# The first eight microseconds: two DMA queues, constant fillers, halved means and one tile turned by DMA instead of PE

## Chip, cores, metric

One core of a Trainium2 chip, one launch. The metric is the device time of a launch in microseconds; the median of several executions is quoted. The kernel takes about 1624 us, and the change touches only its opening, so everything below is about differences of 0.1 to 3 us.

## The reference

Four blocks in a row on x of 2048 x 1024 in bf16: linear attention, a gated bilinear block, and both again. Only the start matters here:

```python
x = A_x                                             # 2048 x 1024
x = x + _A_ref(_layernorm(x, axis=-1), A_wqkv, A_wo)
# _A_ref: qkv = x @ wqkv; phi(q), phi(k); ... ; o @ wo
```

The kernel cannot do its first useful product before a tile of 128 rows has been loaded, centred, and transposed, and the first slice of the k weights has landed.

## The kernel before

PE computes k = xn @ Wk for tiles of 128 rows; each tile needs 8 weight chunks of 128 rows (256 KB each) and 16 matmuls. Tiles 0 to 3 are the opening. Tile 0 gets its mean on VectorE, tile 1 on ScalarE. Tiles 0 to 2 are turned by PE transposes and copied from PSUM to `xT`; tile 3 is turned by a DMA. Until tile 0 is ready PE does "fillers": 9 matmuls on a zeroed tile, whose results nobody reads.

```python
for c in range(2):                                   # tile 0 in two halves of columns
    load(X[:, 0, c*NB:(c+1)*NB], x_view[:, 0, c*NB:(c+1)*NB])
load_x(1)
for k in range(2): load_k(k, k + 1)                  # k weights by chunks; load() is SyncE's queue
load_x(2)
...
nc.vector.memset(xT[3][:, 0, :], 0.0)
def idle(n):                                         # the fillers
    for _ in range(n):
        nc.tensor.matmul(out=zps[:, 0, :], lhsT=xT[3][:, 0, 0:P], rhs=xT[3][:, 0, :], ...)
... (cut)
idle(9)
ln_stats(0)                                          # 2 bn_stats + aggregate on VectorE
centre(0, stat[0][0][:, 0:1])
nc.scalar.activation(out=junk[:], in_=X[:, 1, :], func=ACT.Copy, scale=1.0/D, accum_out=mean1[:])
turn_pe(0, 2)
take(nc.vector.tensor_copy, 0, 0, 0, 2); take(nc.scalar.copy, 0, 1, 2, 8)
centre(1, mean1[:])
k_part(0, 0, 1)                                      # k_part(tile, first chunk, end chunk)
turn_pe(1, 4)
take(nc.vector.tensor_copy, 1, 0, 0, 4); take(nc.scalar.copy, 1, 1, 4, 8)
ln_stats(2); centre(2, ...)
k_part(1, 0, 1)
... (cut: chunks 1 and 2) ...
turn_pe(2, 8)
... (cut)
```

## Time and profile before

| what | value |
|---|---|
| median before the prediction, 3 executions | 1623.66 us (1623.5 to 1624.11) |
| all executions of this study but the profiled one, 50 of them | mean 1623.70 us (1623.1 to 1624.91) |
| the profiled execution | 1624.31 us, of which 1622.4 us is the span of its trace |

The first lines of the page of the kernel before. PE is the TensorE matmul row; a busy PE is not a PE at its peak (from 9 to 11 us, shown below, it reads 2.00 of 2.00 us busy with 17 instructions in one trace and with 7 in another).

```profile
span 1622.4 us, 18054 instructions
PE 1609.2 (99%) x7718; PEld 735.2 (45%) x7869; DVE 615.5 (38%) x941; ACT 283.8 (17%) x383; POOL 54.5 (3%) x135
```

So PE is the limit, and a change of the opening is worth what it moves PE's unbroken run forward. The chain of waits in the first 24 us says where that run begins. Columns: start us, us, what.

```profile
1.65 3.85 DMA X<-in_A_x_dram
...
5.51 1.16 ACT junk L422 x2
...
6.70 0.50 DVE R L398
...
7.24 0.41 PE pt L411 x4
...
7.68 0.44 DVE xT L414
...
8.16 2.33 PE ps L198 x10
10.49 0.45 PE pt L411 x8
```

Read it so: tile 1 of X (the DMA) landed at 5.49 us, ScalarE took its mean, VectorE centred it, PE turned it, VectorE copied it, and from 8.16 us PE does not wait again in this stretch. Tile 2's 8 transposes take 0.45 us of PE in the middle of that run.

PE's instructions in order of time in the same kernel (start us, us, line, operation, count, and in brackets the idle time before and what ended it):

```profile
1.17 4.02 PE L168 MATMUL ps<-xT 128*128 128x512 bf16 x9 [1.17 <-DVE xT L163]
5.17 0.68 PE L411 MATMUL pt<-ident,R 128*128 128x128 bf16 x8
6.23 0.59 PE L198 MATMUL ps<-W,xT 128*128 128x512 bf16 x2 [0.38 <-DMA W<-in_A_wqkv_dram]
7.24 0.62 PE L411 MATMUL pt<-ident,R 128*128 128x128 bf16 x8 [0.42 <-DVE R L398]
8.16 2.33 PE L198 MATMUL ps<-W,xT 128*128 128x512 bf16 x10 [0.30 <-DVE xT L414]
```

One thing is easily overlooked: the fillers start 0.427 us apart, the matmuls from 8.16 us on 0.216 us apart, with the same shape. PE's clock doubled in between; the trace's record of it is at 5.33 us, and there the distance of the transposes falls from 0.107 to 0.056 us.

### The profile page before, as it was taken

How to read it: one execution, taken by the hardware profiler on the slowest of the kernel's cores; microseconds unless marked ns; L12 is line 12 of the kernel's file. 1: busy time of each engine (PE TensorE's matmuls, PEld its weight loads, DVE VectorE, ACT ScalarE, POOL GpSimd, SP SyncE). 2: the span in 40 equal slices, each digit the busy share in tenths (PEclk: the TensorE clock that was granted, in tenths of full speed). 3: DMA queues.
4: the chain of work that ended last, by engine and by line, in shares of the span. 5: the costliest groups of instructions: out<-in, count | busy, mean ns of one | idle time of the engine just before them, and what ended most of it. 6: DMA issues, size and time to landing. Idle time of an engine off the chain costs nothing.

```text
span 1622.4 us, 18054 instructions
## 1 busy us (share of the span) xinstructions
PE 1609.2 (99%) x7718; PEld 735.2 (45%) x7869; DVE 615.5 (38%) x941; ACT 283.8 (17%) x383; POOL 54.5 (3%) x135
## 2 busy tenths in 40 slices
PE   9999999999999999999999999999999999999999
PEld 4444444444444444444444444444444444444444
DVE  6799853212311321243245798432123113211111
ACT  5523201101110110011045222011011101101110
POOL 2100000000000000010000000000000000000000
PEclk9999999999999999999999999999999999999999
DMA  7324856511650452142420349555235406511400
GB/s 233 59 72 98 241 162 175 162 53 55 167 168 0 141 160 89 52 155 63 90 56 1 78 98 252 156 163 163 71 101 172 130 20 175 162 65 65 156 0 26
DMA packets 235775, 182.84 MB, mean 113 GB/s; under 512 B 101296, under 2 KB 216496, under 8 KB 235696
## 3 DMA queue, kind: packets, MB, share of 16 engines
q1 hardware_dynamic: 235696, 181.69, 38.9%
q8 instruction: 61, 1.00, 0.3%
q14 instruction: 18, 0.15, 0.0%
HBM read 153.09 MB, written 4.19 MB: 97 GB/s over the span
## 4 chain that ended last, share of the span: by engine, by line
PE 99%; issue 1%; DMA 0%; DVE 0%; ACT 0%; SPq 0%
PE ps L198 50%; PE ps L529 47%; PE ps L556 1%; PE kv L312 0%; DMA X<-in_A_x_dram 0%; PE pm L337 0%; ACT junk L422 0%; PE pt L411 0%; SPq L109 0%; DVE R L398 0%; DVE xT L414 0%; DVE X L537 0%; PE ps L337 0%
## 5 line engine op out<-in xcount | busy, mean ns | idle before, releaser
L529 PE MATMUL ps<-xT,R 128*128 128x512 bf16 x2380 | 525.8, 379 | 2.8
L529 PEld LDWEIGHTS <-R 128*128 128x128 bf16 x2432 | 237.9, 98 | 287.0
L533 DVE TENSOR_TENSOR R<-gs,ps 128x512 bf16<-128x512 f32 x224 | 154.0, 687 | 533.4 <-ACT gs L532 533.4
L198 PEld LDWEIGHTS <-R 128*128 128x128 bf16 x2248 | 220.0, 98 | 265.2
L532 ACT COPY gs<-ps 128x512 f32<-128x512 f32 x224 | 131.3, 586 | 1040.2 <-PE ps L529 1017.2
L529 PE MATMUL ps<-xT,W 128*128 128x512 bf16 x1134 | 250.6, 379 | 0.9
L198 PEld LDWEIGHTS <-xT 128*128 128x128 bf16 x1536 | 149.2, 98 | 180.6 <-issue 2.1
L198 PE MATMUL ps<-W,xT 128*128 128x512 bf16 x996 | 223.1, 379 | 2.3 <-DMA W<-in_A_wqkv_dram 0.4
L529 PEld LDWEIGHTS <-W 128*128 128x128 bf16 x1152 | 112.7, 98 | 135.9
L198 PE MATMUL ps<-W,R 128*128 128x512 bf16 x732 | 170.1, 379 | 0.8
L537 DVE TENSOR_TENSOR X<-X,ps 128x1024 bf16<-128x1024 bf16 (+3 forms) x34 | 39.4, 1159 | 335.7 <-PE ps L198 282.6
L198 PE MATMUL ps<-PQ,R 128*128 128x512 bf16 x486 | 111.6, 379 | 0.6
L198 PE MATMUL ps<-R,R 128*128 128x512 bf16 x506 | 111.8, 379 | 0.4
L198 PE MATMUL ps<-R,xT 128*128 128x512 bf16 x502 | 110.3, 379 | 0.5
L177 DVE BATCH_NORM_STATS2 st<-X 128x6 f32<-128x512 bf16 x128 | 81.9, 682 | 2.1 <-DMA X<-in_A_x_dram 1.9
L203 ACT ACTIVATE e<-ps 128x1024 bf16<-128x1024 f32 x56 | 57.4, 1025 | 140.2 <-PE ps L198 134.7
L181 POOL TENSOR_SCALAR ve<-mv 128x1 f32<-128x1 f32 x64 | 16.8, 262 | 1328.1 <-DVE mv L179 1328.1
L198 PE MATMUL ps<-GL,R 128*128 128x512 bf16 x241 | 57.6, 379 | 0.2
L198 PE MATMUL ps<-xT,R 128*128 128x512 bf16 x240 | 57.5, 379 | 0.2
L382 DVE TENSOR_TENSOR X<-X,ps 128x1024 bf16<-128x1024 bf16 x32 | 38.5, 1212 | 25.5 <-PE ps L198 25.5
L188 DVE TENSOR_SCALAR R<-X,mv,rstd 128x1024 bf16<-128x1024 bf16 x64 | 33.9, 542 | 24.0 <-POOL rstd L183 24.0
L207 DVE TENSOR_SCALAR e<-e 128x1024 bf16<-128x1024 bf16 x64 | 27.0, 422 | 40.0 <-ACT e L203 40.0
(65 smaller groups left out, 446.6 us busy)
## 6 DMA issues: line engine op xcount, KB each, us to landing
R<-in_B_w_gate_dram SPq DMA_DIRECT2D x38, 1024.0 KB, 5.5
R<-in_B_w_up_dram SPq DMA_DIRECT2D x38, 1024.0 KB, 7.4
W<-in_B_w_gate_dram SPq DMA_DIRECT2D x18, 1024.0 KB, 5.4
W<-in_B_w_up_dram SPq DMA_DIRECT2D x18, 1024.0 KB, 7.3
W<-in_A_wqkv_dram SPq DMA_DIRECT2D x10, 1024.0 KB, 6.0
W<-in_B_w_down_dram SPq DMA_DIRECT2D x6, 1024.0 KB, 11.1
PQ<-in_B_w_down_dram SPq DMA_DIRECT2D x4, 1024.0 KB, 7.9
X<-in_A_x_dram SPq DMA_DIRECT2D x15, 256.0 KB, 6.3
```

Of the source, the lines that this page charges most:

```text
L177: nc.vector.bn_stats(out=st[:, c, :], in_=X[:, t, c * NB:(c + 1) * NB])
L181: nc.gpsimd.tensor_scalar(out=ve[:], in0=mv[:, 1:2], scalar1=1e-5, scalar2=None, op0=ALU.add)
L188: nc.vector.tensor_scalar(out=dst, in0=X[:, t, :], scalar1=mv[:, 0:1], scalar2=rstd[:], op0=ALU.subtract, op1=ALU.mult)
L198: nc.tensor.matmul(out=ps[:, n, :], lhsT=lhsT, rhs=rhs[:, n * NB:(n + 1) * NB], start=start, stop=stop)
L203: nc.scalar.activation(out=e[:], in_=flat(ps), func=ACT.Exp, **sc)
L207: nc.vector.tensor_scalar(out=e[:], in0=e[:], scalar1=1.0, scalar2=EPS, op0=ALU.min, op1=ALU.add)
L382: nc.vector.tensor_tensor(out=X[:, t, :], in0=X[:, t, :], in1=flat(ps), op=ALU.add)
L529: nc.tensor.matmul(out=ps[:, n, :], lhsT=w[:, k, j * P:(j + 1) * P], rhs=xT[g % 2][:, k, :], start=(k == 0), stop=(k == KD - 1))
L532: nc.scalar.copy(out=gs[:], in_=ps[:, 0, :])
L533: nc.vector.tensor_tensor(out=hT[:, f, :], in0=gs[:], in1=ps[:, 1, :], op=ALU.mult)
L537: nc.vector.tensor_tensor(out=X[:, t, a:b], in0=X[:, t, a:b], in1=ps, op=ALU.add)
L556: nc.tensor.matmul(out=ps[:, 0, 0:b - a], lhsT=hT[:, f, tl * P:(tl + 1) * P], rhs=wd[f][:, a:b], start=(f == 0), stop=(f == KF - 1))
```

## The change

Intent: get the first products earlier. SyncE's and ScalarE's DMA queues start loading at once; tile 0's mean is split over two engines; the fillers read a constant and so need no memset; a product of tile 0 fills the wait for tile 1's copy; tile 2 costs PE no transposes any more.

```diff
-    for c in range(2):
-        load(X[:, 0, c * NB:(c + 1) * NB], x_view[:, 0, c * NB:(c + 1) * NB])
+    for eng, h in ((nc.sync, 0), (nc.scalar, 64)):
+        eng.dma_start(out=X[h:h + 64, 0, :], in_=x_view[h:h + 64, 0, :])
+    nc.scalar.dma_start(out=wkv[:, 0, :], in_=wqkv_v[:, 0, D:2 * D])
     load_x(1)
-    for k in range(2):
+    for k in range(1, 3):
         load_k(k, k + 1)
     load_x(2)
-    for k in range(2, 4):
-        load_k(k, k + 1)
+    load_k(3, 4)
     load_x(3)
@@ fillers: memset of xT[3] gone
-            nc.tensor.matmul(out=zps[:, 0, :], lhsT=xT[3][:, 0, 0:P], rhs=xT[3][:, 0, :], start=True, stop=True)
+            nc.tensor.matmul(out=zps[:, 0, :], lhsT=nc.const_aps.tensor(1.0, [P, P], BF16),
+                             rhs=nc.const_aps.tensor(1.0, [P, NB], BF16), start=True, stop=True)
@@ opening
             idle(9)
-            ln_stats(0)
-            centre(0, stat[0][0][:, 0:1])
+            mean_by_halves(0, 0)      # ScalarE sums columns 0:512, VectorE 512:1024
+            centre_by_halves(0, 0)    # subtracts both partial means
@@ (cut: mean of tile 1, transposes of tiles 0 and 1 and their copies, as before)
-            ln_stats(2)
-            centre(2, stat[2][0][:, 0:1])
-            k_part(1, 0, 1)
-            for k in range(1, 3):
-                for t in range(2):
-                    k_part(t, k, k + 1)
-            turn_pe(2, 8)
+            k_part(0, 1, 2)
+            k_part(1, 0, 2)
+            for t in range(2):
+                k_part(t, 2, 3)
+            mean_by_halves(2, 2)
+            centre_by_halves(2, 2)
+            turn(XN[:, 2, :], 0, 2)   # DMA transpose
@@ (cut: statistics of tiles 0 to 2 and the other k_parts come later)
```

More of the change, by code (lines that the diff above doesn't have):

```diff
@@ L161, in flat @@
         return ps[:].rearrange("p a b -> p (a b)")
-    nc.vector.memset(xT[3][:, 0, :], 0.0)
     zps = mm_tile()
@@ L400, in layer_A, with turn_pe, mean_by_halves, centre_by_halves @@
             pts = {}
-            def turn_pe(t, cut):
-                for h, (i, j) in enumerate(((0, cut), (cut, KD))):
-                    if i == j:
-                        continue
-                    tag, bufs = ("mm", 3) if h else ("kv0", 1)
-                    pt = psum.tile([P, KD, P], BF16, tag=tag, bufs=bufs, name="pt")
-                    pts[t, h] = pt
-                    for k in range(i, j):
-                        nc.tensor.transpose(out=pt[:, k, :], in_=XN[:, t, k * P:(k + 1) * P], identity=ident[:])
+            def turn_pe(t, h, a, b):
+                tag, bufs = ("mm", 3) if t and h else (f"kv{h}", 1)
+                pts[t, h] = psum.tile([P, KD, P], BF16, tag=tag, bufs=bufs, name="pt")
+                for k in range(a, b):
+                    nc.tensor.transpose(out=pts[t, h][:, k, :], in_=XN[:, t, k * P:(k + 1) * P], identity=ident[:])
             def take(copy, t, h, a, b):
                 copy(out=xT[0][:, a:b, t * P:(t + 1) * P], in_=pts[t, h][:, a:b, :])
+            part = small.tile([P, 4], F32, tag="part", bufs=1, name="part")
             mean1 = small.tile([P, 1], F32, tag="mean1", bufs=1, name="mean1")
             junk = small.tile([P, D], BF16, tag="eb", bufs=3, name="junk")
+            def mean_by_halves(t, i):
+                nc.scalar.activation(out=junk[:, 0:NB], in_=X[:, t, 0:NB], func=ACT.Copy, scale=1.0 / D,
+                                     accum_out=part[:, i:i + 1])
+                nc.vector.tensor_scalar(out=junk[:, NB:D], in0=X[:, t, NB:D], scalar1=1.0 / D, scalar2=0.0,
+                                        op0=ALU.mult, op1=ALU.add, accum_out=part[:, i + 1:i + 2])
+            def centre_by_halves(t, i):
+                nc.vector.tensor_scalar(out=XN[:, t, :], in0=X[:, t, :], scalar1=part[:, i:i + 1],
+                                        scalar2=part[:, i + 1:i + 2], op0=ALU.subtract, op1=ALU.subtract)
             idle(9)
-            ln_stats(0)
-            centre(0, stat[0][0][:, 0:1])
+            mean_by_halves(0, 0)
+            centre_by_halves(0, 0)
             nc.scalar.activation(out=junk[:], in_=X[:, 1, :], func=ACT.Copy, scale=1.0 / D, accum_out=mean1[:])
-            turn_pe(0, 2)
+            turn_pe(0, 0, 0, 2)
             take(nc.vector.tensor_copy, 0, 0, 0, 2)
+            turn_pe(0, 1, 2, 8)
             take(nc.scalar.copy, 0, 1, 2, 8)
@@ L427, in layer_A @@
             k_part(0, 0, 1)
-            turn_pe(1, 4)
+            turn_pe(1, 0, 0, 4)
             take(nc.vector.tensor_copy, 1, 0, 0, 4)
+            turn_pe(1, 1, 4, 8)
             take(nc.scalar.copy, 1, 1, 4, 8)
-            ln_stats(2)
-            centre(2, stat[2][0][:, 0:1])
-            k_part(1, 0, 1)
-            for k in range(1, 3):
-                for t in range(2):
-                    k_part(t, k, k + 1)
-            turn_pe(2, 8)
+            k_part(0, 1, 2)
+            k_part(1, 0, 2)
             for t in range(2):
-                k_part(t, 3, 4)
-            take(nc.scalar.copy, 2, 0, 0, 8)
+                k_part(t, 2, 3)
+            mean_by_halves(2, 2)
+            centre_by_halves(2, 2)
+            turn(XN[:, 2, :], 0, 2)
             ln_stats(3)
@@ L446, in layer_A @@
                 load_x(t)
-            ln_stats(1)
+            for t in range(3):
+                ln_stats(t)
+            for k in range(3, 6):
+                for t in range(2):
+                    k_part(t, k, k + 1)
             for t in range(2):
-                k_part(t, 4, 6)
-            k_part(0, 6, 8)
-            k_part(2, 0, 6)
-            for t in range(1, 3):
                 k_part(t, 6, 8)
+            k_part(2, 0, 8)
             k_part(3, 0, 8)
```

## The prediction

> **What bounds the kernel.** The page gives PE 1609.2 of 1622.4 us busy. The chain of waits is PE all the way from 8.16 us; before that: two SP issues (0.40, 0.42 us), tile 1 of X in flight from 1.65 to 5.49 us, ScalarE's mean of it 1.16, centring 0.50, PE transposes 0.41, copy to xT 0.44. So the change can touch about 8 us of 1624 plus PE work it removes later. Two per cent (32 us) is out of reach either way.
>
> **What changes, costed.**
> 1. Tile 0's statistics (two bn_stats at 0.68 us, an aggregate at 0.21, done at 4.59 us) become half a row each on ScalarE and VectorE. ScalarE's 128x1024 pass took 1.06 us plus 0.19 for the accumulator[...]. Tile 0 is centred near 4.3 us instead of 5.12. Off the chain: PE waits for tile 1.
> 2. The fillers read a constant: they start near 0.75 us instead of 1.17 and end near 4.6. Tile 0's transposes move up 0.5 us. Off the chain too.
> 3. Half of tile 0 and weight chunk 0 go out on ScalarE's queue, so SP's next issues move up 0.47 us. But chunk 0, which landed behind tile 1 (6.19 against 5.49), now shares the engines with it[...]. Tile 1 lands when about 768 KB have moved rather than 512. Estimate: 5.35 us (4.9 to 5.8), 0.15 us on the chain.
> 4. Chunk 1 of tile 0 is put ahead of tile 1's first product, so two matmuls (0.43 us) fill the wait for the copy to xT. On the chain: 0.45 us.
> 5. Tile 2 is turned by DMA: 8 PE transposes leave at 10.49 us. On the chain: 0.45 us.
>
> Sum: about 1.05 us.
>
> **What may give it back.** (a) Tile 2's transpose: the one before took 3.2 us from issue to landing on an empty queue; issued at 9.6 us it queues behind the last weight chunks (before, to 12.59 us), lands near 13.7, needed near 14.05. (b) The second half of the q weights landed at 22.14 us, needed 22.86; PE gains 1 us on it, the load only 0.3 to 0.4. Slack about zero. I subtract 0.2 us for both. (c) Tile 0's later rstd (about 14.4 us) delays phi; PSUM buffers should still be free in time.
>
> **Prediction.** 1623.66 - 0.85, about 1622.8 us; 8 in 10 between 1621.8 and 1623.7. Faster by over 2%: 0.003; within 2%: 0.994; slower by over 2%: 0.003.
>
> **What would show it.** Timeline: fillers start below 0.9 us; tile 0's transposes near 4.6; tile 1's mean near 5.35; after tile 1's transposes PE runs on without a gap, from about 7.55 us instead of 8.16; 16 transposes instead of 24; k of tiles 0 and 1 ends 1.1 us earlier; PE waits for tile 2's transpose or the q weights under 0.5 us. Past 25 us both traces alike, shifted.
>
> **What would make it wrong.** Tile 1 landing over 6 or under 4.8 us through the two queues; ScalarE's issues holding up its table load and half mean; the DMA transpose landing after 14.5 us; a PSUM buffer chosen so that k of tile 2 waits for phi of tile 0 (over 2 us).

Two passages are cut from it, each marked, because no trace here shows what they say: in step 1 the formula and the estimate for ScalarE's half mean, in step 3 the rule that stood behind the sharing of the engines. Step 1 is off the chain, and 0.15 + 0.45 + 0.45 is 1.05 us, less 0.2 for (a) and (b) the 0.85 subtracted. (The sharing itself was seen afterwards: from 2.0 to 3.0 us in the changed kernel ScalarE's queue kept the 16 DMA engines busy for 62.1% and SyncE's for 34.1% of the time.)

## The result

The changed kernel: 1625.66 us median of 5 (1623.88 to 1626.43) against 1623.66 of 5 (1623.1 to 1624.11). The ratio is 1.001, 95% interval 0.9997 to 1.0024. A ratio here is the mean time of one kernel's fast runs over that of the other's in the same rounds, so it is not quite the ratio of the medians that I quote. By that interval, "the same"; but the median lies 2 us outside my range on the wrong side, and the spread of five executions grew from 1.0 to 2.6 us. A second set of five (the run after_again below) gave 1624.69 (1623.01 to 1627.23). Mean of the ten: 1625.07, that is 1.4 us more than before.

The page of the changed kernel, same two lines:

```profile
span 1624.6 us, 18204 instructions
PE 1619.7 (100%) x7861; PEld 735.8 (45%) x7861; DVE 616.2 (38%) x944; ACT 283.9 (17%) x386; POOL 54.0 (3%) x135
```

PE looks busier, 1619.7 us against 1609.2. Most of that is not work: some matmul records were missing in the trace of before (7718 of them against 7861, although this kernel has 8 transposes fewer). The chain of waits answers better:

```profile
0.72 0.58 SPq L137
...
1.36 4.90 DMA X<-in_A_x_dram
...
6.37 1.16 ACT junk L429 x2
...
7.55 0.50 DVE R L398
...
8.09 1.04 PE pt L407 x8
9.13 15.00 PE ps L198 x61
```

Two things changed against before. Tile 1 was issued 0.29 us earlier and landed 0.77 us later (6.26 us against 5.49). And from the transposes on PE runs without a stop, as I had forecast, so the shape of the chain is right. PE's instructions show what is wrong with that unbroken run:

```profile
0.76 4.00 PE L167 MATMUL ps<-const-bfloat16-1.0 128*128 128x512 bf16 x9 [0.76 <-PEq L635]
5.45 1.03 PE L407 MATMUL pt<-ident,R 128*128 128x128 bf16 x8 [0.70 <-DVE R L423]
6.28 1.06 PE L198 MATMUL ps<-W,xT 128*128 128x512 bf16 x2
8.09 1.04 PE L407 MATMUL pt<-ident,R 128*128 128x128 bf16 x8 [0.75 <-DVE R L398]
8.92 11.32 PE L198 MATMUL ps<-W,xT 128*128 128x512 bf16 x43
```

The two products at 6.28 us take 1.06 us here and took 0.59 before; 8 transposes take 1.03 and 1.04 us instead of 0.68 and 0.62. PE is still at half clock. How long? The busy time of each engine in a stretch from 9 to 11 us gives the number of PE instructions that ran in it (the x after PE), first before, then after:

```profile
9.00:11.00 2.00, 2.00 (x17) 1.14 (x16) 1.93 (x5) 0.03 (x1) 1.09 (x2) 1.00 1.06 406
```

```profile
9.00:11.00 2.00, 2.00 (x7) 0.68 (x5) 1.36 (x5) 1.21 (x3) 0.00 (x0) 1.00 1.05 403
```

PE is "busy" 2.00 of 2.00 us in both, with 17 instructions (8 of them short transposes) before and 7 after. The distance of matmul starts falls from 0.427 to 0.216 us only at 12.7 us. (The column before the last two, the granted clock, reads 1.00 in both: the trace of the changed kernel has no clock record at all, and the view then shows full clock. The distance of equal matmuls is the thing to trust.)

The sum for this pair of traces, from start times of PE: tile 1's transposes begin at 8.09 instead of 7.24 us, +0.85. From there to the next product 0.83 instead of 0.92 us, -0.09: the copy wait is filled (-0.47), but the 8 transposes are slow (+0.38). From that product (the third of the kernel) to the tenth after it 4.04 instead of 2.61 us, +1.42: half clock costs +1.87, the eight transposes that left give -0.45. Together 2.18 us. The first ScalarE instruction for tile 4 comes 2.19 us later, and 1.57 ms into the kernel the shift is still 2.18 us, so nothing later adds to it. Before, then after:

```profile
25.65 1.11 ACT L203 ACTIVATE e<-ps,rstd 128x1024 bf16<-128x1024 f32 x1 [1.33 <-PE ps L198]
```

```profile
27.84 1.11 ACT L203 ACTIVATE e<-ps,rstd 128x1024 bf16<-128x1024 f32 x1 [1.33 <-PE ps L198]
```

This instruction is the marker used below: its time against 25.65 us is called the shift of a trace.

### The profile page after: what moved, and what is told of

Read it like the earlier page. It is cut to its first block, busy times and chain, and to the rows that moved or that the text cites. A ratio compares the mean times of both kernels' runs of the same rounds, so it can differ in the third digit from the quotient of the medians.

```text
span 1624.6 us, 18204 instructions
## 1 busy us (share of the span) xinstructions
PE 1619.7 (100%) x7861; PEld 735.8 (45%) x7861; DVE 616.2 (38%) x944; ACT 283.9 (17%) x386; POOL 54.0 (3%) x135
## 4 chain that ended last, share of the span: by engine, by line
PE 99%; DMA 0%; ACT 0%; DVE 0%; SPq 0%; issue 0%; ACTq 0%
PE ps L198 50%; PE ps L536 48%; PE ps L563 1%; DMA X<-in_A_x_dram 0%; PE kv L312 0%; PE pm L337 0%; ACT junk L429 0%; PE pt L407 0%; SPq L137 0%; DVE R L398 0%; DVE X L544 0%; PE ps L337 0%; ACTq L429 0%
## 5 line engine op out<-in xcount | busy, mean ns | idle before, releaser
L198 PE MATMUL ps<-W,xT 128*128 128x512 bf16 x1024 | 227.2, 382 | 0.0
```

What stands on the lines that cost most here:

```text
L198: nc.tensor.matmul(out=ps[:, n, :], lhsT=lhsT, rhs=rhs[:, n * NB:(n + 1) * NB], start=start, stop=stop)
```

## The experiments

Theories. **Clock:** the fillers now end at 4.55 us and tile 0's transposes start at 5.45; with 0.9 us idle in between, PE's work no longer suffices to bring up the clock, or does so only in some executions. **Data:** a constant of ones, read again and again, does not count as activity. **Loads:** the two queues make tile 1 late, and that is all. Some of the expectations below named a rule for how much PE work brings up the clock. No trace here shows that rule, so it is cut from them (the cuts are marked).

17 runs were made, two of them repeats of a kernel, all with 5 executions and all correct; "before" in a row is the median of nine executions of the kernel before in the same call. The calls ran on different chips; the medians of before differ by up to 0.44 us between them. Names that begin with a derive from the changed kernel, those with b from the kernel before. "Full clock" is when the trace first records it (in the first set of after, which has no record, when the distance of matmul starts falls to 0.216 us); "tile 1" when its DMA landed.

| run | edit | median (range) | before | full clock | tile 1 | shift |
|---|---|---|---|---|---|---|
| after, first set | none | 1625.66 (1623.88-1626.43) | 1623.66 (5) | 12.7 | 6.26 | +2.18 |
| after_again | none | 1624.69 (1623.01-1627.23) | 1623.65 | 3.37 | 6.37 | +0.07 |
| a_idle11 | 11 fillers | 1624.29 (1623.36-1625.62) | 1623.69 | 4.43 | 6.32 | +0.03 |
| a_idle14 | 14 fillers | 1624.18 (1622.88-1624.43) | 1623.65 | 6.10 | 5.64 | -0.63 |
| a_idle5 | 5 fillers | 1624.92 (1624.47-1626.96) | 1623.65 | 8.94 | 6.06 | +0.21 |
| b_const9 | constant fillers | 1623.18 (1623.14-1624.20) | 1623.69 | 3.78 | 4.37 | -1.12 |
| b_idle5 | 5 fillers | 1625.07 (1624.68-1625.32) | 1623.68 | 9.06 | 4.80 | +0.27 |
| b_loads | loads of after | 1625.43 (1624.29-1626.22) | 1623.69 | 10.51 | 4.55 | +1.65 |
| b_rows | tile 0 by rows, one queue | 1624.80 (1624.50-1625.95) | 1623.45 | 5.57 | 5.02 | +0.54 |
| b_x0act | tile 0 by rows, two queues | 1624.65 (1624.51-1625.58) | 1623.45 | 4.90 | 5.08 | +0.09 |
| b_w0act | chunk 0 on ScalarE's queue | 1625.86 (1624.83-1626.16) | 1623.45 | 9.77 | 6.33 | +1.31 |
| a_idle11_loads | 11 fillers, loads of before | 1622.99 (1622.47-1623.85) | 1623.69 | 5.58 | 4.98 | -0.96 |
| a11l_again | the same again | 1623.74 (1623.11-1624.11) | 1623.68 | 6.74 | 4.15 | -1.14 |
| a_idle14_loads | 14 fillers, loads of before | 1623.86 (1623.06-1624.39) | 1623.89 | 3.70 | 4.35 | -1.25 |
| a14l_pe2 | that, tile 2 by PE | 1623.61 (1623.38-1624.26) | 1623.89 | 6.28 | 4.49 | -0.09 |
| a14l_order | that, tile 1's product first | 1623.65 (1623.20-1624.31) | 1623.89 | 3.78 | 4.97 | -0.88 |
| a14l_cols | that, tile 0's column halves on two queues | 1623.69 (1623.02-1624.24) | 1623.89 | 6.11 | 4.53 | -0.62 |
| best1 | 11 fillers, loads of before, tile 3 later | 1623.51 (1622.88-1624.46) | 1623.65 | 5.37 | 5.44 | +0.16 |

A shift is one execution, the one profiled; the median is of five. Where they disagree, that execution was not the typical one, and this turned out to matter. The zero of the shift is one execution too, and a slow one: 1624.31 us, where the mean of before is 1623.70. None of the intervals excludes 1 (they are about 0.25% wide); what I read from times are whole groups of executions against each other.

### Fillers and clock

**after_again: the changed kernel as it is.**

> The changed kernel as it is, once more, to see whether its wide spread is a lottery between two states of the clock. [...] about half of the executions warm up near 4 to 5 us and take 1623.5 to 1624.7, the others stay cold to 11 or 12.7 us and take 1625.5 to 1626.5; the trace of the profiled one agrees with its own time. Otherwise: one cloud around 1625.

```profile
0.76 3.38 PE L167 MATMUL ps<-const-bfloat16-1.0 128*128 128x512 bf16 x9 [0.76 <-PEq L635]
5.46 0.62 PE L407 MATMUL pt<-ident,R 128*128 128x128 bf16 x8 [1.33 <-DVE R L423]
6.14 0.60 PE L198 MATMUL ps<-W,xT 128*128 128x512 bf16 x2
8.19 0.62 PE L407 MATMUL pt<-ident,R 128*128 128x128 bf16 x8 [1.45 <-DVE R L398]
```

The same program, with its fillers and first transposes starting at the same times, but full clock from 3.37 us: the transposes take 0.62 us instead of 1.04. Tile 1 landed 0.11 us later than in the first trace, and yet the marker came at 25.72 us instead of 27.84. So half clock cost about 2.1 us in the first one, and the state differs from execution to execution. The times of the five, spread over 4.2 us, show no clear gap by themselves, but the record tells more: it gives a mean granted clock for every execution, profiled or not. Time before the first clock record counts there as full clock, so a late first grant does not show (all five of b_idle5 below read 1.000), but a recorded stretch at half clock does. Of the ten executions of the changed kernel four read 0.999 or 0.998 (0.001 of a span of 1623 us is 1.6 us of clock lost, so by estimate, from figures rounded to 0.001, about 3 and 6 us at half clock). These four and the first profiled one, at half clock to 12.7 us, took 1625.44 to 1627.23 us, 1626.15 on the average; the other five took 1623.01 to 1624.74, 1623.99 on the average. So half of the executions are known to have run at half clock for a while, and they took 2.2 us longer than the others, which fits the 2.1 us between the two traces. (That the others were at full clock early is seen in a trace for one of them only.) None of the 45 executions of before in the later calls reads under 1.000.

**a_idle11, a_idle14 and a_idle5: the number of fillers.**

```diff
-            idle(9)
+            idle(11)      # a_idle11;  14 in a_idle14;  5 in a_idle5
```

> The changed kernel with 11 fillers instead of 9, so that they reach to about 5.45 us, where tile 0's transposes start (in the changed kernel the fillers end at 4.55 us and PE is idle for 0.9 us). Gap theory: PE at full clock before 6 us (matmul starts 0.216 us apart instead of 0.427), and the time falls by about 2 us against the changed kernel, to about 1623.5 (tile 1 still lands late, near 6.3 us). Data theory (a broadcast constant of ones doesn't count as work for the clock): still cold to about 12 us, time near 1625.5. Loads theory (only the late tile 1 matters): no change, near 1625.5.

> The changed kernel with 14 fillers, which reach past 6 us and end before tile 1 is ready (8.1 us in the changed kernel). [...] PE is at full clock before 7 us in every execution[...]: median near 1624.0, all five within 1623 to 1624.7, none above 1625. If fillers don't matter: like the changed kernel, 1623.9 to 1626.4.

> The changed kernel with 5 fillers, which end at 2.9 us, so that PE is idle for 2.5 us before tile 0's transposes. [...] median near 1626.3, all five at or above 1625.5, and the trace cold (0.427 us a matmul) until 10.5 to 12.7 us. If the fillers don't matter: like the changed kernel, 1625.0 with the same spread.

With 11 and 14 fillers the profiled executions were at full clock at 4.43 and 6.10 us. The ten times have a mean of 1624.07 against 1625.07 of the ten of the changed kernel: 1.0 us for two or five matmuls whose results nobody reads. The median with 11, 1624.29, missed the forecast 1623.5; one of its five was still at 1625.62, and its granted clock reads 0.999, so 11 do not keep every execution from half clock. With 14 none was above 1624.43, as expected. Only in the trace with 14 can the added fillers have had a part: its full clock, at 6.10 us, came after the 4.55 us at which nine fillers end in the changed kernel, that of 11 before it. With 5 fillers no execution was below 1624.47, but the median, 1624.92, is well short of the 1626.3 that I forecast and no different from what I expected if fillers don't matter (1625.0), so this run alone decides nothing. Its trace came to full clock at 8.94 us, not 10.5 or later: my estimate of how much PE work it takes was too strict.

**b_const9: the constant in the kernel before; b_idle5: fewer fillers in the kernel before.**

```diff
# b_const9: the filler lines of the change, and the memset gone; nothing else
# b_idle5:
-            idle(9)
+            idle(5)
```

> The kernel before with only the fillers changed to the constant, 9 of them: they start at 0.76 instead of 1.17 us and end at 4.6, 0.55 us before tile 0's transposes. Gap theory: cold well past 5.3 us in some or all executions, so slower by 1 to 3 us and with a wider spread than before (up to 1626). Data theory: cold in all, 1625 to 1627 with little spread. Loads theory: the same time as before, 1623.7.

> The kernel before with 5 fillers instead of 9 and nothing else changed; they end at 3.3 us, 1.9 us before tile 0's transposes. If PE's idle time in the first 6 us decides the clock: cold until 8.2 to 11.6 us, loads as before (tile 1 at 4.4 to 5.5 us), and slower by 0.7 to 2.5 us, median near 1625, spread over 1 us. If the fillers only pass the time: 1623.7, spread under 1 us.

b_const9 came to full clock at 3.78 us, while still in its fillers: the data theory is out. It did not turn cold either, as the clock theory had held possible; 1623.18 is even 0.5 below before, of which I make nothing, because its tile 1 landed at 4.37 us in the trace (see below). b_idle5 is the cleanest run of all: nothing but four fillers fewer in the kernel before, tile 1 early (4.80), full clock at 9.06 us, and all five executions (1624.68 to 1625.32) above all nine of before (up to 1623.95). Median +1.4 us, at the forecast 1625 (the spread, 0.6 us, is smaller than forecast). PE's instructions in its trace, to be set beside those of before above:

```profile
1.17 2.31 PE L168 MATMUL ps<-xT 128*128 128x512 bf16 x5 [1.17 <-DVE xT L163]
5.02 1.04 PE L411 MATMUL pt<-ident,R 128*128 128x128 bf16 x8 [1.54 <-DVE R L398]
7.86 2.91 PE L198 MATMUL ps<-W,xT 128*128 128x512 bf16 x10
```

The same 8 transposes take 1.04 instead of 0.68 us, the same 10 products 2.91 instead of 2.33. The fillers do not just pass the time; they buy the clock (5.33 us with nine, 9.06 with five).

How much PE work does it take? These traces do not show it. Between the end of the fillers (the last one's start plus 0.427 us) and tile 0's transposes PE stood idle for 0.9 us in the first trace of the changed kernel (4.55 to 5.45), 1.1 in b_loads, 1.7 in b_idle5 and 2.5 in a_idle5, and full clock came at 12.7, 10.51, 9.06 and 8.94 us: late in all four, but not later after a longer hole. And the same program, with the same start of fillers and transposes, had it at 3.37 us in after_again. So no threshold can be read from them. In the kernel before, the fillers ran to 5.0 us and the transposes followed at 5.17, and no execution of 50 took longer than 1624.91.

### Loads

**b_loads: only the loads of the change.**

```diff
# in the kernel before: the load lines of the change, nothing else
```

> The kernel before with only the order and queues of the opening loads changed. Loads theory: slower by 1 to 2 us, with tile 1 landing near 6.3 us instead of 5.49 and PE at full clock from about 5.3 us. Gap theory: fillers still end at 5.0 us, so tile 1's 0.8 us alone shows: about 1624.4, unless the longer wait for tile 1 also leaves PE cold.

1625.43, 1.7 us slower, but not as expected: tile 1 landed early (4.55 us), and chunk 0, which comes from the other queue, at 7.17. In the changed kernel it was the other way round (chunk 0 at 4.48, tile 1 at 6.26). In these two traces whichever of the two comes second lands after 6.2 us. Tile 0 was complete at 3.95 us instead of 3.38, its transposes began at 6.08 instead of 5.17, and with that hole after the fillers (5.0 to 6.08 us) PE stayed cold to 10.51 us. So the loads act twice: directly, and through the clock.

How do two queues share? SyncE's and ScalarE's issues in the changed kernel (start us, us, queue):

```profile
0.72 0.57 ACTq L137 DMA_DIRECT2D X<-in_A_x_dram  x1
0.72 0.58 SPq L137 DMA_DIRECT2D X<-in_A_x_dram  x1
1.32 0.60 ACTq L138 DMA_DIRECT2D W<-in_A_wqkv_dram  x1
1.36 0.83 SPq L109 DMA_DIRECT2D X<-in_A_x_dram  x1
```

Before, three issues took 0.40, 0.42 and 0.42 us. Both halves of tile 0, chunk 0 and tile 1 were issued by 2.19 us on two queues and by 2.55 us on one; tile 1 itself by 2.19 against 2.07 us, so for the tile that matters nothing was saved (with halves by columns on two queues it was issued by 1.62 us, a14l_cols). And what the DMA engines moved from 3.00 to 3.75 us, by queue (q10 is ScalarE's, q1 SyncE's; packets, MB, share of the engines), in the changed kernel and then in b_loads, which has the same load lines:

```profile
q10 hardware_dynamic: 102, 0.21, 88.1%
q1 hardware_dynamic: 8, 0.00, 1.2%
```

```profile
q1 hardware_dynamic: 107, 0.21, 94.2%
q10 hardware_dynamic: 18, 0.02, 8.8%
```

In the changed kernel tile 1 was fully issued at 2.19 us and hardly moved until chunk 0 was nearly done; in b_loads chunk 0 waited for tile 1. So in this stretch the loads of 256 KB took turns almost as wholes (102 packets to 8, and 107 to 18, most of them rows of 2 KB). They do not always: in b_w0act both queues moved side by side (from 2.0 to 3.0 us 83 packets on ScalarE's, 66 on SyncE's). What decides whose turn comes first is not shown; in all nine traces with two queues the queue whose first issue began first, by 1 to 9 ns, also landed its first load first. The longer issue of tile 1 (0.83 instead of 0.42 us) is no sign of a busy second queue: b_x0act, where ScalarE issues nothing after its half of tile 0, has it too (0.81), and with halves by columns it is absent (0.42 in b_w0act, 0.44 in a14l_cols).

**b_rows, b_x0act, b_w0act and a14l_cols: one part of the loads at a time.**

```diff
# b_rows: both halves of tile 0 by rows, on SyncE
+    for h in (0, 64):
+        load(X[h:h + 64, 0, :], x_view[h:h + 64, 0, :])
# b_x0act: the same, rows 64:128 on nc.scalar.  b_w0act: column halves on SyncE, only chunk 0 on nc.scalar
# a14l_cols (on a_idle14_loads): column half 0 on nc.sync, column half 1 on nc.scalar
```

> The kernel before with tile 0 loaded in two halves of 64 rows instead of two halves of columns, both still on SP's queue. If it is the halving by rows that made tile 0 land at 3.9 instead of 3.3 us and everything behind it later: tile 0 complete near 3.9, tile 1 near 6, time up by 0.5. If it is the second queue: as before (3.3, 4.4 to 5.5, 1623.7).

> As the one with rows, but with the second half on ScalarE's queue and nothing else moved. If two queues at the start cost time by themselves: issues of 0.57 us instead of 0.40, tile 0 complete at 3.9 us, tile 1 later than 5.5, time up by 0.3 to 1. If only chunk 0 on the second queue hurts: tile 0 at 3.3 or earlier, tile 1 at 5.0, time 1623.3.

> The kernel before with only weight chunk 0 moved to ScalarE's queue. If chunk 0 takes tile 1's place in the engines: whichever of the two comes second lands at 6.2 us or later, and the time is up by 0.3 to 1.5. If sharing is harmless: tile 1 at about 5.3, chunk 0 too, time 1623.5.

> The same version with tile 0's two column halves on two queues, nothing else moved. If the halving by rows is the cost: issues of 0.40 us, tile 0 complete by 3.1 us, tile 1 at 5 us or earlier, time within 0.2 of that version. If two queues are the cost: issues of 0.57 us, tile 0 complete near 3.9 us, tile 1 later by 0.3 to 0.8.

| loads | issue of a half of tile 0 | tile 0 complete | tile 1 | chunk 0 |
|---|---|---|---|---|
| before: columns, one queue | 0.40, 0.42 | 3.38 | 5.49 | 6.19 |
| b_rows: rows, one queue | 0.58, 0.58 | 4.46 | 5.02 | 6.14 |
| b_x0act: rows, two queues | 0.56, 0.59 | 4.02 | 5.08 | 5.79 |
| a14l_cols: columns, two queues | 0.40, 0.39 | 3.99 | 4.53 | 6.34 |
| b_w0act: columns, chunk 0 beside them | 0.40, 0.44 | 4.43 | 6.33 | 4.05 |
| after: rows, two queues, chunk 0 | 0.57, 0.58 | 3.92 | 6.26 | 4.48 |

The question that I had put, rows or queue, has the answer "both, and neither makes tile 1 late". A half by rows took 0.56 to 0.59 us to issue, on one queue as on two. Two queues, even by columns, complete tile 0 at 3.99 us instead of 3.38. But with chunk 0 in its old place tile 1 lands at 5.1 us or before. Of the seven traces with chunk 0 on ScalarE's queue six (the two of the changed kernel, a_idle11, a_idle14, a_idle5, b_w0act) have tile 1 at 5.64 to 6.37 us; in the seventh, b_loads, it came first and chunk 0 at 7.17. The nine traces with the first four loads of before have tile 1 at 4.15 to 5.49. b_w0act, in which nothing but the queue of chunk 0 is changed, is the slowest run by its median: 2.4 us above before, where I had forecast 0.3 to 1.5, and all five executions above all nine of before; tile 0 and tile 1 are both late there and full clock came at 9.77 us. In b_rows and b_x0act tile 1 was early and the kernel nevertheless 1.2 to 1.35 us slower by the median; there the chain of both traces runs through the late tile 0 to PE: before's bn_stats needs columns 0:512 of all rows, so it cannot start on half of the rows. Whether half clock adds to it in their other executions is not known (one of b_rows, 1625.95, reads 0.999).

### What became of the two gains

**a_idle11_loads, a_idle14_loads and a11l_again: the change without its two faults.** (11 or 14 fillers, and the load lines of before.)

> The changed kernel with 11 fillers and the loads of before, all on SP's queue. Gap and loads theories together: tile 1 lands near 5.5 us, PE at full clock from about 5 us, PE without gaps from about 7.6 us, and my two remaining gains (0.45 us of filled copy wait, 0.45 us of transposes) show: about 1622.7, faster than before by 0.9. Data theory: cold, 1624.5 or more.

> The changed kernel with 14 fillers and the loads of before: the clock warms in every execution and tile 1 lands at 4.4 to 5.5 us. If the explanation is right this beats both kernels: about 1623.0, 0.6 below before, with a spread under 1.5 us and no execution above 1624.5. If something else in the changed kernel costs: 1623.7 or more.

> The changed kernel with 11 fillers and the loads of before, once more (first time 1622.99 against 1623.69). If it is better than both kernels: median 0.4 to 0.9 below the kernel before of the same call, none of five above 1624. If that was luck: within 0.2 of it.

The first gave 1622.99, 0.7 below before and near the forecast 1622.7; the repetition 1623.74 against 1623.68, by its own forecast the sign that the first was luck; the one with 14 fillers 1623.86 against 1623.89, where I had forecast 1623.0. Over the 15 executions the mean is 1623.53, and 1623.78 over those of before of the same calls (the mean of the three calls' means): 0.25 us remain of 0.9. There is no version here that beats the kernel before by an amount worth claiming.

**a14l_pe2 and a14l_order: one gain taken away each.**

```diff
# a14l_pe2
-            turn(XN[:, 2, :], 0, 2)
+            turn_pe(2, 0, 0, 8)                       # after chunk 5
+            take(nc.scalar.copy, 2, 0, 0, 8)
# a14l_order
-            k_part(0, 1, 2)
-            k_part(1, 0, 2)
+            k_part(1, 0, 1)
+            for t in range(2):
+                k_part(t, 1, 2)
```

> The same with tile 2 turned by PE again (8 transposes after weight chunk 5, copied by ScalarE). If the DMA transpose is worth what its 8 transposes took in the trace: 0.45 us slower than that version. If PE was waiting for the weight chunks or for tile 2 at that place anyway: no difference.

> The same version with tile 1's first product ahead of chunk 1 of tile 0 again, as before. If filling the copy wait is worth its 0.45 us: 0.45 slower, with PE idle for 0.3 us between tile 1's transposes and its first product. If PE then waits for weight chunk 4 (it did, 0.35 us, in the trace with 11 fillers): only 0.1 slower.

The times show nothing (1623.61 and 1623.65 against 1623.86). The traces do. a14l_pe2 and a14l_cols both started their long run at nearly the same time (8.04 and 7.95 us) and neither waited in it. Their markers, first with tile 2 by PE, then by DMA:

```profile
25.56 1.11 ACT L203 ACTIVATE e<-ps,rstd 128x1024 bf16<-128x1024 f32 x1 [1.33 <-PE ps L198]
```

```profile
25.03 1.11 ACT L203 ACTIVATE e<-ps,rstd 128x1024 bf16<-128x1024 f32 x1 [1.33 <-PE ps L198]
```

0.53 us, less the 0.09 of their start: 0.44, the size that I had read from before. And in a14l_order PE's first product of tile 1 came 0.92 us after the first transpose (6.81 to 7.73 us), in a_idle11_loads 0.45 us after (6.82 to 7.27). Both gains are real. They are lost elsewhere, as the chain of a_idle14_loads shows:

```profile
4.96 5.40 DMA W<-in_A_wqkv_dram
10.35 0.04 issue
10.39 15.70 PE ps L198 x72
```

PE had begun its run at 6.79 us there, and stood still once for chunk 2 and once for chunk 4, which landed at 10.35 us. In the profiled execution of a_idle11_loads it waited 0.35 us for the same chunk (10.63 us), and so its marker is only 0.08 us ahead of that of a14l_order, with tile 1 landing alike (4.98 and 4.97 us). In b_const9, with tile 1 as early (4.37 us), the old order first used chunk 4 at 10.52 us, when it had landed at 10.15; the new order used it at 10.39. So when tile 1 comes early, both orders come to chunk 4 at about the same time, and earlier or fewer PE instructions buy a wait. And tile 1 does come early: of all traces with the old loads, the one from which I made my prediction has it latest (5.49; the others 4.15 to 5.44).

**best1: the weights ahead of tile 3.**

```diff
# a_idle11_loads with this order of loads:
+    load_x(1); load_k(0..2); load_x(2); load_k(3..5); load_x(3); load_k(6..7)
```

> The changed kernel with 11 fillers, all loads on SP's queue, and tile 3 loaded behind weight chunks 3 to 5 instead of ahead of chunk 4. In the same kernel with the old order PE ran from 7.27 us but stood still for 0.35 us at 10.3 us until chunk 4 landed (10.63). Here chunk 4 should land 0.65 us earlier and that stop should go: about 0.3 us below that kernel's 1622.99, so 1622.6. If weights aren't the next limit: 1623.0.

1623.51 against 1623.65: missed. In its trace tile 3 landed at 12.02 us. Its statistics stand ahead of those of tiles 0 to 2 in VectorE's order, so tile 0's came late, with it the exponential of tile 0, and PE had no free PSUM buffer for tile 3:

```profile
17.55 1.12 ACT R L204
18.66 0.04 issue
18.70 5.56 PE ps L198 x25
```

This is the risk (c) that I had named and that did not strike in the changed kernel itself; one moved load was enough to bring it about. (In this execution chunk 1 was late too, at 8.05 us, and chunk 4 landed at 10.70 us, no earlier than with the old order, so this trace does not test what I had meant to test.)

### The account

Of the 1.4 us by which the ten executions of the changed kernel exceed those of before: 1.0 is the mean of the ten with more fillers against them (1625.07 to 1624.07); 0.54 is what the old loads gave on top (1624.07 to 1623.53); -0.25 is what remains for the other parts. These are successive differences and must add up: the sum, 1.29, is 0.1 us short only because before had 1623.78 in the calls of the last term and 1623.65 in those of the changed kernel. So the sum checks nothing. The split by clock bears it out: half of the ten executions, 2.2 us slower, make 1.1 us of the mean, and the other half lies 0.3 us above before, which is 0.54 less 0.25.

The scatter is large. Estimated from that of single executions (up to 4.2 us apart in the changed kernel), the standard errors are 0.5 us for the first term and 0.3 for the second, so each alone is about two of them from zero. The causes rest on b_idle5 and b_w0act, each with all five executions above all nine of before, and on the traces. Part of the noise lies elsewhere: six of the 19 traces, a_idle14 and after_again among them, lose another 0.1 to 0.5 us near 980 us, which no part of the change explains. And a part of each time lies outside the span of the trace: 1.8 to 1.9 us in most runs, 2.1 in b_x0act and b_w0act, 1.9 to 2.0 in the three with more fillers and old loads. So 0.3 us of the loss of those two and 0.1 us of the lost gain are not in PE's run at all, and no trace shows where they are.

## Why the prediction was wrong

- **Bound, chain, PE limit:** right. Past 25 us the two traces are alike but for the shift.
- **Step 1, tile 0's statistics:** the duration was right (ScalarE's half took 0.63 + 0.19 us, close to the estimate). "Tile 0 is centred near 4.3 us" was not: 5.40, because tile 0 landed at 3.92.
- **Step 2, the failed one:** "The fillers read a constant: they start near 0.75 us instead of 1.17 and end near 4.6. ... Off the chain too." The times are right to 0.05 us; "off the chain" is wrong. They end 0.9 us before the next PE work, and half of the executions are then known to run at half clock for a while: 2.1 us lost in the profiled one, 1.0 us on the average of ten. "Tile 0's transposes move up 0.5 us" is the other side of that hole: they came at 5.45 us instead of 5.17, with the late tile 0. The early end of the fillers alone did no harm (b_const9, 1624.20 us at most), and the late tile 0 did harm with the old fillers too (b_loads, hole from 5.0 to 6.08 us). So the loads of before alone, with nine constant fillers, might have cured the changed kernel; that was not run.
- **Step 3, the other failed one:** "Estimate: 5.35 us (4.9 to 5.8), 0.15 us on the chain." 6.26 us. The term that was mis-sized is the time for 768 KB. Whether the queues share the engines or follow each other, tile 1 is the last of the first 768 KB unless it goes ahead of chunk 0 (it landed at 6.26 us, chunk 0 at 4.48); and in the trace that I predicted from, the last of them (chunk 0) landed at 6.19 us, not at 5.35. SyncE's issue of tile 1 moved up by 0.29 us instead of 0.47, because a half by rows took 0.58 us to issue. I had named "landing over 6 us" as a thing that would make me wrong. Executions with 11 or 14 fillers but these loads averaged 0.54 us more than those with the old ones.
- **Steps 4 and 5, the fill and tile 2 by DMA:** right in mechanism and size where they can be seen (0.47 and 0.44 us). Mis-sized in the sum: of 0.9 us about 0.25 remains with the clock and the loads repaired, because my baseline trace had the latest tile 1 of all those with its loads, and with an early one the weights are the next limit. Its execution took 1624.31 us, 0.65 above the median from which I subtracted the gains.
- **Risks (a) and (b), tile 2's transpose and the q weights:** neither made PE wait in the changed kernel, so the 0.2 us that I took off was not needed.
- **Step 3's side effect, ScalarE's table load behind two issues:** it ended at 3.23 us, before tile 0 landed. Harmless.

What stays open: how much PE work brings up the clock; what decides which of two queues goes first; whether the old loads alone would have kept the clock; the shares of the two clock states beyond ten executions; and the distribution of tile 1's landing, which would need many more traces.

## What to carry to other kernels

Work that kept PE busy before the data came was part of the critical path here even though nobody reads its result: four fillers fewer cost 1.4 us (b_idle5). Let it reach to the next real PE work without a hole, and check the clock by the distance of equal matmuls (0.427 or 0.216 us here), not by busy time. A DMA put on a second queue went ahead of what the first one had to move in the changed kernel (102 packets to 8) and behind it in b_loads (18 to 107), so leave what the chain waits for alone at the head. And before summing gains from one trace of a kernel that waits for DMAs, look at how much those landings vary (tile 1 came at 4.15 to 5.49 us with the same first four loads): the next limit may lie just behind.
